# Moving 256 rows of the last weight onto other DMA engines in a single-core decode kernel

## The chip, the core and the metric

The kernel runs on one core of a Trainium2 chip. The core has five compute engines that the profile names: PE (TensorE, matrix multiplies; PEld is its weight load), DVE (VectorE), ACT (ScalarE), POOL (GpSimd) and SP (SyncE, here only used to issue DMAs). Sixteen DMA engines move data between HBM and the core's memory. A DMA load is issued by one compute engine's queue and is cut into packets, one per partition row here; the packets are spread over the DMA engines and each of these works its own share down.

The metric is the device time of one execution in microseconds (us). The median of three runs of the kernel before is 193.46 us (193.40 to 193.61).

## The reference

One token of eight sequences goes through an attention block with a cached window, and then through a small MLP block:

```python
x = A_x
h = x + _A_ref(_layernorm(x, axis=-1), A_k_cache, A_v_cache, A_wq, A_wo)
h2 = h + _B_ref(_layernorm(h, axis=-1), B_w1, B_w2, B_w3, B_w4)
```

`_A_ref` projects x (8 x 512) by wq (512 x 4096) to 32 heads, takes the last 2048 cached positions of K and V (8 sequences, 8 key heads, 128 wide, bf16), does a softmax attention and multiplies by wo (4096 x 512). `_B_ref` has a first part with w1 and w2 that shifts tokens; with one token the shifted terms are all zero, so what is left is

```python
h2 = _gelu(_layernorm(x1, axis=-1) @ w3) @ w4      # w3: 512 x 1792, w4: 1792 x 512
return x1 + h2
```

## The kernel before

Each compute engine has its own list of operations (class `Engine`, lines 39 to 70); `op` appends one with the semaphore values that it waits for. Order on an engine is the order of the Python calls; engines meet through semaphores alone. The helper `dma` (line 197) appends a load to an engine's list.

**Loads.** SP issues nearly everything, in one order: wq (4 MB), then 32 loads of 2 MB of K and V into a ring of 8 buffers, then wo in four loads of 1 MB (`sem_wo`), w3 in two of 896 KB, and w4 in four. A K or V load waits until the ring buffer that it overwrites was read (`taken`). w3 and w4 go into ring buffers as well (`w3_sb`, `w4_sb`, buffers W3S and W4S) and wait for `w_free`. Each load of 128 partitions puts eight packets on each of the sixteen DMA engines, and each engine works through SP's loads in order. w4 has 14 chunks of 128 rows, loaded as 8, 3, 2 and 1 chunks (`w4_chunks`, `w4_ends`, `sem_w4`). ACT issues one small load, x (line 215).

**Attention.** For each of 64 quarters PE transposes K (`pe_T`, L325), ACT and DVE copy the transposes out (L334, L336), PE forms the scores (`pe_QK`, L345). After eight quarters comes a softmax; POOL spreads the probabilities over four columns (L384), PE transposes them (L394), and multiplies by V (`pe_PV`, L445). The V product lags the scores by 20 quarters.

**Tail.** When the last V is used, PE reorders the result (L534), and `pe_wo` multiplies by wo in four steps, each of which waits for its load (L548). Between the steps `stream(n)` (L596) issues n multiplications whose result nobody reads. Then come sums over the features (L685 to L700), `pe_w3` in two halves (L710; second half waits for the second w3 load), a scaling on DVE (L738) and a gelu on ACT (L741), both in two parts of 8 and 6 chunks. `pe_w4` (L755) adds w4 chunk by chunk, as the four loads land, into an accumulator which `pe_fin` (L747) has opened. DVE and ACT copy out (L775, L776), and SP stores (L779).

**POOL's list.** It begins with memsets and an iota (L204 to L213), has the 30 spreads of L384, and ends with the memset `e_uz` of L684, which clears the buffer `uT` that pe_w3's operand is written into.

Of the kernel before, what the change touches and what calls it, by code (L numbers as in the profile page):

```python
# [11 lines left out]
B = 8  # L12
D = 512
# [9 lines left out]
FC = F // 128  # L23
KC = D // 128
EPS = 1e-5

NS = 8
NKT = 3
# [5 lines left out]
NWO = 4  # L34
# [33 lines left out]
def bass_sequential_preLN__sliding_block_cached__mixer_s_mlp__decode_kernel(  # L68
# [23 lines left out]
    with es:  # L92
        sb = lambda shape, dtype, name: es.enter_context(nc.sbuf_tensor(name, shape, dtype))
        ps_t = lambda shape, dtype, name: es.enter_context(nc.psum_tensor(name, shape, dtype))
        S = lambda name: es.enter_context(nc.semaphore(name))
# [4 lines left out]
        ident_b = sb([128, 128], dt.bfloat16, "ident_b")  # L100
# [7 lines left out]
        x_sb = sb([B, D], dt.bfloat16, "x_sb")  # L108
# [8 lines left out]
        QH, RW = H // 8, 8  # L117
# [4 lines left out]
        ring = sb([128, NS, NCQ * DH], dt.bfloat16, "ring")  # L122
        W3S, W4S = (2 * 2 * NB) % NS, (2 * 2 * NB + 1) % NS
        w3_sb = ring[:, W3S, 0:KC * F].rearrange("p (k f) -> p k f", k=KC)
        w4_sb = ring[:, W4S, 0:FC * D].rearrange("p (k n) -> p k n", k=FC)
        kT_sb = sb([128, NKT, 16 * 128], dt.bfloat16, "kT_sb")
# [3 lines left out]
        P4_sb = sb([128, 512, 4], dt.bfloat16, "P4_sb")  # L130
# [17 lines left out]
        half = sb([128, 2], dt.float32, "half")  # L148
# [19 lines left out]
        r2 = sb([128, B], dt.float32, "r2")  # L168
        xb = sb([128, NH], dt.float32, "xb")
        fin = sb([128, NH], dt.float32, "fin")  # L170
        uT = P4_sb[:, 0:64, :].rearrange("p (n w) k -> p n (w k)", n=KC)
        g_x = sb([128, FC * B], dt.float32, "g_x")
# [15 lines left out]
        oT_ps = sm[:, 480:512]  # L188

        sem_r = [S(f"sem_r{i}") for i in range(NS)]  # L190
        sem_wo = [S(f"sem_wo{i}") for i in range(NWO)]
        sem_x, sem_wq, sem_out = (S(n) for n in ("sem_x", "sem_wq", "sem_out"))
        sem_w3 = [S(f"sem_w3{i}") for i in range(2)]
        sem_w4 = [S(f"sem_w4{i}") for i in range(4)]
        PE, AC, DV, PO, SP = (Engine(S(n)) for n in ("s_pe", "s_act", "s_dve", "s_pool", "s_sp"))

        def dma(eng, dst, src, sem, *waits):
            def f(e):
                e.dma_start(dst, src).then_inc(sem, 16)  # L199
            eng.op(f, *waits, inc=False)  # L200


        X = (sem_x, 16)
        e_scr = PO.op(lambda e: e.memset(scratch[:], 1.0))  # L204
        PO.op(lambda e: e.memset(eps1[:], EPS))
        e_eps = PO.op(lambda e: e.memset(eps2[:], EPS * EPS))
        e_iota = PO.op(lambda e: e.iota(iota_f[:], [[1, 128]], base=0, channel_multiplier=-1,
# [4 lines left out]
        e_xz = PO.op(lambda e: e.memset(xlnT[:], 0.0))  # L212
        e_qz = PO.op(lambda e: e.memset(qwin[:], 0.0))  # L213
        e_warm = AC.op(lambda e: e.activation(scratch[:, 1:2], scratch[:, 0:1], ACT.Exp), e_scr)
        dma(AC, x_sb[:], A_x.rearrange("b s d -> (b s) d"), sem_x)

        e_idb = DV.op(lambda e: e.tensor_single_scalar(ident_b[:], iota_f[:], 0.0, ALU.is_equal), e_iota)
        e_idf = DV.op(lambda e: e.tensor_single_scalar(ident_f[:], iota_f[:], 0.0, ALU.is_equal))
# [324 lines left out]
        def pe_wo(n, *waits):  # L543
            def f(e):
                for q in range(n * (QH // NWO), (n + 1) * (QH // NWO)):
                    for r in range(RW):
                        for nb in range(KC):
                            ins = e.matmul(hT_ps[:, nb * NW:(nb + 1) * NW], wo_v[:, q, r, cols[nb]],  # L548
                                           oR_t[:, r * NW + q * B:(r + 1) * NW + q * B], start=(q == 0 and r == 0 and nb == 0),
                                           stop=(q == QH - 1 and r == RW - 1), skip_group_check=True)  # L550
                return ins
            e_wo.append(PE.op(f, (sem_wo[n], 16), e_exp[NB - 2], *waits))

        assert NG == 64 and LPV == 20
        at = {4 * (w + 1) + 2: w for w in range(SHARE)}
# [34 lines left out]
            if p >= 7 + LQK + 7 and (p - 7 - LQK - 7) % 8 == 0:  # L590
                softmax_5((p - 7 - LQK - 7) // 8)

        def stream(n):
            def f(e):
                for _ in range(n):
                    ins = e.matmul(O2_ps[:, :], ident_b[:, :], kT_sb[:, (NG - 1) % NKT, 0:512], start=True, stop=True)  # L596
                return ins
            if n:
                PE.op(f, e_acc[NV - 4])
# [37 lines left out]
        pick_rest(14, 1)  # L637
        finish(13)
        pick_rest(14, 2, 3)
        stream(4)  # L640
        pv(60)
        finish(14)
        pv(61, 62, 63)

        e_oR = reorder()
        stream(3)
        for n in range(NWO):
            pe_wo(n, e_oR, e_oz)
            stream((0, 4, 4, 1)[n])


        dma(SP, wq_v, A_wq.rearrange("(p k) n -> p k n", k=KC), sem_wq)
        for l in loads:
            what, b, j = l
            if what == "wo":
                n, qh = b, QH // NWO
                dma(SP, wo_v[:, n * qh:(n + 1) * qh].rearrange("p q r n -> p q (r n)"),
                    A_wo[n * qh * 128 * RW:(n + 1) * qh * 128 * RW, :].rearrange("(q p r) n -> p q (r n)", p=128, r=RW),
                    sem_wo[n], e_q)
                continue  # L660
            n = place[l]
            src = (A_k_cache if what == "k" else A_v_cache)[b, 4 * j:4 * (j + 1), W0:SK, :].rearrange(
                "h (p c) d -> p h (c d)", p=32)
            free = taken[quads[n - NS]] if n >= NS else None
            dma(SP, ring[:, n % NS, :], src, sem_r[n % NS], free)


        w_free = [taken[quads[n - NS]] for n in (len(quads), len(quads) + 1)]
        for a, sem in enumerate(sem_w3):
            dma(SP, w3_sb[:, 2 * a:2 * (a + 1), :].rearrange("p r f -> p (r f)"),  # L670
                B_w3[256 * a:256 * (a + 1), :].rearrange("(p r) f -> p (r f)", r=2), sem, w_free[0])

        FH = 8
        w4_chunks, w4_ends, f0 = [], [], 0
        for r, sem in zip((8, 3, 2, 1), sem_w4):
            lo = len(w4_chunks)
            w4_chunks += [slice(f0 + i, f0 + 128 * r, r) for i in range(r)]
            dma(SP, w4_sb[:, lo:lo + r, :].rearrange("p r n -> p (r n)"),
                B_w4[f0:f0 + 128 * r, :].rearrange("(p r) n -> p (r n)", r=r), sem, w_free[1] if lo == 0 else None)
            w4_ends.append(lo + r)  # L680
            f0 += 128 * r
        assert len(w4_chunks) == FC

        e_uz = PO.op(lambda e: e.memset(uT, 0.0), e_PT[LAST, 3])  # L684
        e_d = DV.op(lambda e: e.tensor_tensor(v3(hd[:, :]), hT, v3(xc[:, :]), ALU.add), e_wo[-1], e_xc[0])  # L685
        st1, st2 = sm[:, 0:NH], O_ps[:, 64:64 + NH]
        e_st1 = PE.op(lambda e: e.matmul(st1, ones_f[:, :], hd[:, :], start=True, stop=True), e_d)
# [12 lines left out]
        e_hc = DV.op(lambda e: e.scalar_tensor_tensor(v3(hc[:, :]), bc(msum), -1.0 / D, v3(hd[:, :]),  # L700
                                                      ALU.mult, ALU.add))

        y_ps, NY = [kbank[0], kbank[2]], (64, 32)

        def pe_w3(half, lo, hi, *waits):
            def f(e):
                for fc in range(lo, hi):
                    n, f = divmod(fc, FH)
                    for kc in (2 * half, 2 * half + 1):
                        ins = e.matmul(y_ps[n][:, f * NY[n]:(f + 1) * NY[n]], w3_sb[:, kc, w4_chunks[fc]],  # L710
                                       uT[:, kc, 0:NY[n]], start=(kc == 0 and f == 0), stop=(kc == KC - 1),
                                       skip_group_check=True)
                return ins
            return PE.op(f, *waits)
        pe_w3(0, 0, FC, e_u, (sem_w3[0], 16), e_scale[LAST, 1], e_acc[NV - 2])
        stream(1)
        e_y = [pe_w3(1, 0, FH, (sem_w3[1], 16)), pe_w3(1, FH, FC)]

        e = AC.op(lambda e: e.activation(s2[:, :], vsum[:, :], ACT.Sqrt, bias=eps2[:, :], scale=(1.0 + EPS) / D), e_vs)  # L719
        e1 = AC.op(lambda e: e.activation(s1[:, :], vsum[:, :], ACT.Sqrt, bias=eps1[:, :], scale=1.0 / D))  # L720
# [9 lines left out]
        def bcf(t, n):  # L730
            a = t[:, :]
            return bass.AP(tensor=a.tensor, offset=a.offset, ap=[a.ap[0], [0, n], [1, B]])

        e_gT = []
        for n in range(2):
            fn = (FH, FC - FH)[n]
            cs = slice(n * FH * B, (n * FH + fn) * B)
            e = DV.op(lambda e, n=n, cs=cs, fn=fn: e.tensor_tensor(v3(g_x[:, cs]),   # L738
                y_ps[n][:, 0:fn * NY[n]].rearrange("p (f w) -> p f w", w=NY[n])[:, :, 0:B], bcf(r2, fn),
                                                                   ALU.mult), e_y[n], e_r2)  # L740
            e_gT.append(AC.op(lambda e, cs=cs: e.activation(gT[:, cs], g_x[:, cs], ACT.Gelu_apprx_tanh), e))  # L741
        z_ps = S_ps[1]

        def rows(e, w, rhs, start=False, stop=False):
# [3 lines left out]
                               stop=stop, tile_position=(0, 64 * a), skip_group_check=True)  # L748
            return ins

        def pe_w4(lo, hi, *waits):
            def f(e):
                for fc in range(lo, hi):
                    for a in range(2):
                        ins = e.matmul(z_ps[64 * a:64 * a + B, 0:256], gT[:, fc * B:(fc + 1) * B],  # L755
                                       w4_sb[:, fc, 256 * a:256 * (a + 1)].rearrange("p (j r) -> p r j", r=2),
                                       start=False, stop=(fc == FC - 1), tile_position=(0, 64 * a), skip_group_check=True)
                return ins
            return PE.op(f, *waits)

# [4 lines left out]
            return ins  # L765

        PE.op(pe_fin, e_fin, e_exp[LAST], e_scale[LAST, 1])
        stream(2)
        for n, hi in enumerate(w4_ends):
            e_z = pe_w4(w4_ends[n - 1] if n else 0, hi, (sem_w4[n], 16), e_gT[0 if hi <= FH else 1])  # L770
        e_out = []
        for a in range(2):
            src = z_ps[64 * a:64 * a + B, 0:256].rearrange("p (r j) -> p r j", r=2)
# [3 lines left out]

        def store(e):
            e.dma_start(out.rearrange("b s d -> (b s) d"), out_sb[:, :]).then_inc(sem_out, 16)  # L779
            e.wait_ge(sem_out, 16)  # L780
        SP.op(store, *e_out, inc=False)

        for eng, e in ((nc.sync, SP), (nc.gpsimd, PO), (nc.scalar, AC), (nc.vector, DV), (nc.tensor, PE)):
# [29 lines left out]
```

## Time and profile before

| what | value |
|---|---|
| median of 3 runs | 193.46 us |
| the profiled execution's own time | 193.76 us |
| its span, first to last instruction | 192.3 us |
| clock granted to TensorE | 1.0 |
| HBM read | 79.18 MB, 412 GB/s over the span |
| PE busy | 159.8 us, 83% of the span |
| POOL busy | 35.8 us, 19% |

The span is shorter than the execution's time by 1.4 us, which lies outside of the first and last instruction. The views that are quoted below are: the page (its slices, its DMA queues, its chain), the chain of work that ended last in order of time, the timeline (start us, duration us, engine, line, operation, output from inputs, how many, and in brackets the idle time before with what ended it), and a table of stretches (busy us of each engine with the count of instructions, granted clock, share of the DMA engines that is busy, GB/s). Beside these views the trace holds a record of every DMA packet, with its start, duration, size and queue, but not the number of its DMA engine.

### The profile page before, as it was taken

How to read it: one execution, taken by the hardware profiler on the slowest of the kernel's cores; microseconds unless marked ns; L12 is line 12 of the kernel's file. 1: busy time of each engine (PE TensorE's matmuls, PEld its weight loads, DVE VectorE, ACT ScalarE, POOL GpSimd, SP SyncE). 2: the span in 40 equal slices, each digit the busy share in tenths (PEclk: the TensorE clock that was granted, in tenths of full speed). 3: DMA queues.
4: the chain of work that ended last, by engine and by line, in shares of the span. 5: the costliest groups of instructions: out<-in, count | busy, mean ns of one | idle time of the engine just before them, and what ended most of it. 6: DMA issues, size and time to landing. Idle time of an engine off the chain costs nothing.

```text
span 192.3 us, 4741 instructions
## 1 busy us (share of the span) xinstructions
PE 159.8 (83%) x2108; PEld 101.8 (53%) x2108; DVE 103.8 (54%) x256; ACT 84.4 (44%) x102; POOL 35.8 (19%) x44
## 2 busy tenths in 40 slices
PE   0028999789998989998999797979998998898795
PEld 0015767567665555655656464646565653366472
DVE  7702656367457654665475546554765456552050
ACT  5002776946744544454444532454445423530040
POOL 8000000350520080008000800052004402400000
PEclk9999999999999999999999999999999999999999
DMA  6999999999999999999999999999999999999992
GB/s 220 436 423 436 433 416 433 426 428 423 436 429 433 429 433 423 426 429 431 433 423 433 429 433 429 429 433 426 424 426 429 429 433 433 423 416 430 418 381 77
DMA packets 6244, 79.47 MB, mean 413 GB/s; under 512 B 705, under 2 KB 849, under 8 KB 1361
## 3 DMA queue, kind: packets, MB, share of 16 engines
q1 hardware_dynamic: 6208, 79.18, 97.0%
q8 instruction: 16, 0.26, 0.5%
q10 hardware_dynamic: 16, 0.01, 0.0%
q14 instruction: 4, 0.02, 0.0%
HBM read 79.18 MB, written 0.01 MB: 412 GB/s over the span
## 4 chain that ended last, share of the span: by engine, by line
DMA 78%; PE 16%; DVE 2%; SPq 2%; issue 1%; ACT 0%
DMA ring<-in_A_k_cache_dram 63%; DMA ring<-in_B_w_dram 16%; PE kT_ps L325 8%; PE O_ps L445 3%; PE S_ps L345 3%; SPq L199 2%; DVE kT_sb L336 1%; PE sm L394 1%; PE sm L496 1%; DVE pT_sb L407 1%; PE S_ps L755 0%; DVE mcol L356 0%; ACT P_sb L775 0%; PE sm L360 0%; PE sm L370 0%
## 5 line engine op out<-in xcount | busy, mean ns | idle before, releaser
L334 ACT ACTIVATE kT_sb<-kT_ps 128x1024 bf16<-128x1024 bf16 x64 | 65.2, 1023 | 65.4 <-PE kT_ps L325 65.4
L325 PE MATMUL kT_ps<-ident_p,ring 128*128 128x128 bf16 x1024 | 68.3, 220 | 9.0 <-DMA ring<-in_A_k_cache_dram 7.6
L336 DVE COPY kT_sb<-kT_ps 128x1024 bf16<-128x1024 bf16 x64 | 44.3, 692 | 48.9 <-PE kT_ps L325 48.9
L325 PEld LDWEIGHTS kT_ps<-ident_p,ring 128*128 128x128 bf16 x1024 | 57.7, 98 | 22.5 <-DMA ring<-in_A_k_cache_dram 10.5
L384 POOL TENSOR_TENSOR P_sb<-P_sb,mask_b 128x512 bf16<-128x512 bf16 x30 | 31.2, 1070 | 129.2 <-ACT P_sb L374 120.1
L445 PE MATMUL O_ps<-ring,pT_sb 128*64 128x512 bf16 x208 | 31.6, 390 | 0.0
L345 PE MATMUL S_ps<-kT_sb,qwin 128*32 128x512 bf16 x256 | 26.0, 390 | 0.0
L345 PEld LDWEIGHTS S_ps<-kT_sb,qwin 128*32 128x32 bf16 x256 | 6.8, 93 | 16.3 <-issue 14.4
L394 PE MATMUL sm<-ident_s,P_sb 128*128 128x128 bf16 x120 | 11.6, 219 | 2.0 <-DVE pT_sb L407 0.7
L407 DVE COPY pT_sb<-sm 128x512 bf16<-128x512 bf16 x28 | 11.6, 415 | 1.1 <-PE sm L394 1.1
L445 PEld LDWEIGHTS O_ps<-ring,pT_sb 128*64 128x64 bf16 x208 | 7.7, 108 | 6.1 <-issue 1.6
L394 PEld LDWEIGHTS sm<-ident_s,P_sb 128*128 128x128 bf16 x120 | 7.7, 97 | 4.5 <-issue 3.6
L480 DVE SCALAR_TENSOR_TENSOR acc<-O_ps,own_f,acc 128x128 f32<-128x128 f32 x24 | 8.4, 350 | 0.8
L268 PE MATMUL S_ps<-wbig,xlnT 128*32 128x512 bf16 x32 | 3.4, 596 | 5.3 <-DMA wbig<-in_A_wq_dram 5.3
L374 ACT ACTIVATE P_sb<-S_ps,negcol 128x512 bf16<-128x512 f32 x8 | 5.5, 687 | 3.0 <-DVE negcol L373 3.0
L254 PE MATMUL sm<-ident_b,xln_b 8*128 8x8 bf16 x4 | 0.3, 174 | 7.6 <-DVE xln_b L223 7.6
L496 PEld LDWEIGHTS sm<-sum_f,acc 128*128 128x128 f32 x20 | 3.0, 188 | 6.3 <-DVE pT_sb L407 3.3
L356 DVE TENSOR_REDUCE mcol<-S_ps 128x1 f32<-128x512 f32 x8 | 5.5, 689 | 1.5 <-PE S_ps L345 1.5
L480 DVE SCALAR_TENSOR_TENSOR iota_f<-O_ps,own_f,iota_f 128x128 f32<-128x128 f32 x15 | 5.2, 348 | 1.5 <-ACT iota_f L483 1.2
L596 PE MATMUL O_ps<-kT_sb,ident_b 128*128 128x512 bf16 x21 | 5.8, 379 | 0.0
L435 DVE TENSOR_TENSOR oT_all<-sm,rL 128x16 bf16<-128x16 f32 x15 | 3.4, 229 | 4.4 <-PE sm L496 4.3
L719 ACT ACTIVATE s<-vsum,eps 128x8 f32<-128x8 f32 x1 | 0.3, 301 | 11.8 <-DVE vsum L699 11.8
(123 smaller groups left out, 109.8 us busy)
## 6 DMA issues: line engine op xcount, KB each, us to landing
ring<-in_A_k_cache_dram SPq DMA_DIRECT2D x16, 2048.0 KB, 30.7
ring<-in_A_v_cache_dram SPq DMA_DIRECT2D x16, 2048.0 KB, 26.8
wbig<-in_A_wq_dram SPq DMA_DIRECT2D x1, 4096.0 KB, 12.3
wbig<-in_A_wo_dram SPq DMA_DIRECT2D x4, 1024.0 KB, 29.9
ring<-in_B_w_dram SPq DMA_DIRECT2D x2, 896.0 KB, 34.9
ring<-in_B_w_dram SPq DMA_DIRECT2D x1, 1024.0 KB, 32.1
ring<-in_B_w_dram SPq DMA_DIRECT2D x1, 384.0 KB, 30.3
ring<-in_B_w_dram SPq DMA_DIRECT2D x1, 256.0 KB, 30.5
```

The costliest lines, as they stand in the source:

```text
L325: ins = e.matmul(kT_ps[m % 3][:, c * 128:(c + 1) * 128], ring[:, s, n * DH:(n + 1) * DH], ident_p[:, :], is_transpose=True)
L334: e_lo[i] = AC.op(lambda e: e.activation(kT_sb[:, i % NKT, 0:1024], kT_ps[2 * i % 3][:, :], ACT.Copy), e_Tlo[i], e_QK.get(i - NKT))
L336: e_hi[i] = DV.op(lambda e: e.tensor_copy(kT_sb[:, i % NKT, 1024:2048], kT_ps[(2 * i + 1) % 3][:, :]), e_Thi[i], e_QK.get(i - NKT))
L345: ins = e.matmul(S_ps[b % 2][32 * h:32 * (h + 1), :], qwin[:, b, 4 * j + h, w0:w0 + 32], kT_sb[:, i % NKT, :].rearrange("p (c h k) -> p h ...
L356: e_max[b] = DV.op(lambda e: e.tensor_reduce(mcol[:, :], S_ps[b % 2][:, :], AX.X, ALU.max), e_QK[8 * b + 7], e_mT.get(b - 1))
L374: e_exp[b] = AC.op(lambda e: e.activation(P_sb[:, :], S_ps[j][:, :], ACT.Exp, bias=negcol[:, j:j + 1], scale=1.0, accum_out=lcol[:, j:j + 1]),
L384: e_sp[b, r] = eng.op(lambda e, r=r, pb=pb, mb=mb: e.tensor_tensor(P4_sb[:, 128 * r:128 * (r + 1), :], pb, mb, ALU.mult), e_exp[b], e_PT.g ...
L394: ins = e.matmul(buf[:, x * 128:(x + 1) * 128], P4_sb[:, 32 * c:32 * (c + 1), :].rearrange("p k h -> p (k h)"), ident_s[:, :], is_transpos ...
L407: e_pT[b, r] = DV.op(lambda e: e.tensor_copy(dst, pT_ps[:, :]), e_PT[b, r], free)
L445: ins = e.matmul(bank(w)[64 * t:64 * (t + 1), :], pT_sb[:, b % NB3, c, 64 * j:64 * (j + 1)], ring[:, s, :].rearrange("p (a c d) -> p c a d ...
L480: e_part[w] = eng.op(lambda e: e.scalar_tensor_tensor(dst, src, own, dst, ALU.mult, ALU.add), e_part[w], e_PV[4 * w + 3])
L596: ins = e.matmul(O2_ps[:, :], ident_b[:, :], kT_sb[:, (NG - 1) % NKT, 0:512], start=True, stop=True)
```

## The change

- **w4, first 128 rows.** Two loads issued by SP (`few(SP, ...)`), each of 64 rows to 8 partitions (8 rows of 1 KB, that is 8 KB, to a partition), with the source's outermost dimension 2, so that each runs on two DMA engines, numbers 0 and 1 by the change's words. They stand behind w3 and ahead of the rest of w4.
- **w4, next 128 rows.** One load issued by POOL (`few(PO, ...)`), 16 partitions of 8 KB, outermost dimension 4: four parts.
- **w4, the other 1536 rows** are loaded by SP as 5, 4, 2 and 1 chunks.
- The 256 rows lie in a ring buffer (`near_sb`) that POOL clears first (`e_nz`); all three loads wait for this memset. Their rows stand on other partitions than the gelu's output has them, so POOL builds selection matrices (`near`: a memset and three copies), `pe_near` (24 small multiplications) sorts the gelu's output, DVE copies it (`gn`), and 16 more multiplications use it with `near_sb`.
- pe_w3, the scaling and the gelu go in three parts (2, 5 and 7 chunks).
- x is loaded by POOL, as the second operation on its list.
- `stream` gets a width: 12, 12, 14, 16 and 4 multiplications of 128 columns stand where 4, 3, 4, 4 and 1 of 512 stood; 3 of 512 in place of 1 between the halves of w3; the 2 ahead of w4 are gone.
- Semaphores of early loads serve late ones again; there are 23 in place of 26.

```diff
-        sem_wo = [S(f"sem_wo{i}") for i in range(NWO)]
-        sem_x, sem_wq, sem_out = (S(n) for n in ("sem_x", "sem_wq", "sem_out"))
-        sem_w3 = [S(f"sem_w3{i}") for i in range(2)]
-        sem_w4 = [S(f"sem_w4{i}") for i in range(4)]
+        sem_x, sem_wq, sem_out, sem_wl, sem_w3l = (S(n) for n in ("sem_x", "sem_wq", "sem_out", "sem_wl", "sem_w3l"))
+        sem_w4l = [S(f"sem_w4{i}") for i in range(3)]
+        full = 16 * (4 * NB // NS)
+        NEAR = (4 * NB - 6) % NS
+        sem_wm = S("sem_wm")
+        w_wo = [(sem_wq, 32), (sem_out, 16), (sem_wl, 16), (sem_wm, 16)]
+        w_w3 = [(sem_r[W3S], full + 16), (sem_w3l, 16)]
+        sem_nw = S("sem_nw")
+        w_w4 = [(sem_r[W4S], full + 16)] + [(sem, 16) for sem in sem_w4l]
...
         e_scr = PO.op(lambda e: e.memset(scratch[:], 1.0))
+        dma(PO, x_sb[:], A_x.rearrange("b s d -> (b s) d"), sem_x)
...
-        dma(AC, x_sb[:], A_x.rearrange("b s d -> (b s) d"), sem_x)
...
-        stream(4)
+        stream(12, 128)
...
-        stream(3)
+        stream(12, 128)
         for n in range(NWO):
             pe_wo(n, e_oR, e_oz)
-            stream((0, 4, 4, 1)[n])
+            stream((0, 14, 16, 4)[n], 128)
...
+        NN, NT = 2, 3
+        side = ring[:, NEAR, :]
+        near_sb = side[:, 0:RW * D].rearrange("p (r n) -> p r n", r=RW)
+        near = side[:, RW * D:RW * (D + 32 * NT)].rearrange("p (r t n) -> p r t n", r=RW, t=NT)
+        e_nz = PO.op(lambda e: e.memset(near_sb, 0.0), taken["k", LAST, 1])
+        def few(eng, p, n, k, f, sem):
+            a = B_w4[f:f + n * RW, :]
+            dma(eng, near_sb[p:p + n].rearrange("p r n -> p (r n)"),
+                bass.AP(tensor=a.tensor, offset=a.offset, ap=[[RW * D, k], [k * RW * D, n // k], [1, RW * D]]), sem, e_nz)
+        few(PO, 64, 16, 4, 128, sem_nw)
+        e = PO.op(lambda e: e.memset(near, 0.0))
...
+        for t in range(2):
+            few(SP, 32 * t, 8, 2, 64 * t, sem_r[NEAR])
+        w4_chunks, w4_ends, f0 = [slice(128 * i, 128 * (i + 1)) for i in range(NN)], [], 128 * NN
+        for r, (sem, _) in zip((5, 4, 2, 1), w_w4):
...
-        e_uz = PO.op(lambda e: e.memset(uT, 0.0), e_PT[LAST, 3])
+        w3_parts = ((0, NN, 64), (NN, w4_ends[0], 64), (w4_ends[0], FC, 32))
+        e_uz = PO.op(lambda e: e.memset(P4_sb[:, 0:80, :], 0.0), e_PT[LAST, 3])
...
-        stream(1)
-        e_y = [pe_w3(1, 0, FH, (sem_w3[1], 16)), pe_w3(1, FH, FC)]
+        stream(3)
+        e_y = [pe_w3(1, n, w_w3[1]) for n in range(3)]
...
+        def pe_near(e):
+            for r in range(RW):
+                for t in range(NT):
+                    n = t // 2
+                    ins = e.matmul(gn_ps[32 * t:32 * (t + 1), r * B:(r + 1) * B], near[:, r, t, :], gT[:, n * B:(n + 1) * B],
+                                   start=True, stop=True, tile_position=(0, 32 * t), skip_group_check=True)
+            return ins
...
-        stream(2)
+        e = PE.op(pe_near, e_gT[0], e_near)
+        e_gn = DV.op(lambda e: e.tensor_copy(gn[0:32 * NT, :], gn_ps), e, e_uz)
         for n, hi in enumerate(w4_ends):
-            e_z = pe_w4(w4_ends[n - 1] if n else 0, hi, (sem_w4[n], 16), e_gT[0 if hi <= FH else 1])
+            e_z = pe_w4(gT, w4_sb, w4_ends[n - 1] if n else NN, hi, w_w4[n], e_gT[1 if n == 0 else 2])
+            if n == 0:
+                pe_w4(gn, near_sb, 0, RW, e_gn, (sem_r[NEAR], full + 32), (sem_nw, 16))
```

## The prediction

> **What bounds the kernel now.** The page first: its span, the slices of DMA, the queues, and the chain that ended last.
>
> ```profile
> span 192.3 us, 4741 instructions
> ...
> DMA  6999999999999999999999999999999999999992
> ...
> q1 hardware_dynamic: 6208, 79.18, 97.0%
> q8 instruction: 16, 0.26, 0.5%
> q10 hardware_dynamic: 16, 0.01, 0.0%
> q14 instruction: 4, 0.02, 0.0%
> ...
> DMA 78%; PE 16%; DVE 2%; SPq 2%; issue 1%; ACT 0%
> ```
>
> The DMA engines are full from the second slice to the last but one, and 78% of the chain is DMA. q1 is SP's loads, q10 is x, q8 and q14 fetch instructions. Next the end of the chain in order of time, then the timeline there.
>
> ```profile
> 159.31 30.47 DMA ring<-in_B_w_dram
> 189.78 0.04 issue
> 189.82 0.61 PE S_ps L755 x6
> 190.43 0.02 issue
> 190.45 0.45 ACT P_sb L775
> ```
>
> ```profile
> 185.57 1.45 PE L710 MATMUL kT_ps<-P_sb,ring 128*128 128x64 bf16 x28 [0.36 <-DMA ring<-in_B_w_dram]
> ...
> 187.99 0.77 PEld L755 LDWEIGHTS S_ps<-ring,gT 128*8 128x8 bf16 x16 [0.59 <-DMA ring<-in_B_w_dram]
> ...
> 189.20 0.21 PEld L755 LDWEIGHTS S_ps<-ring,gT 128*8 128x8 bf16 x6 [0.44 <-DMA ring<-in_B_w_dram]
> 189.82 0.09 PEld L755 LDWEIGHTS S_ps<-ring,gT 128*8 128x8 bf16 x4 [0.41 <-DMA ring<-in_B_w_dram]
> 190.13 0.09 PEld L755 LDWEIGHTS S_ps<-ring,gT 128*8 128x8 bf16 x2 [0.22 <-DMA ring<-in_B_w_dram]
> ```
>
> Each of w4's four loads is waited for; PE starts the last at 190.13. So the end is set by the DMA engine that delivers its share of w4 last. A table of stretches shows that not all are late:
>
> ```profile
> 186.00:186.50 0.50, 0.50 (x12) 0.50 (x11) 0.00 (x0) 0.00 (x0) 0.00 (x0) 1.00 1.02 404
> 186.50:187.00 0.50, 0.50 (x18) 0.47 (x18) 0.23 (x1) 0.00 (x0) 0.00 (x0) 1.00 0.60 242
> ...
> 187.50:188.00 0.50, 0.40 (x4) 0.01 (x4) 0.00 (x0) 0.05 (x1) 0.00 (x0) 1.00 0.52 197
> ...
> 188.50:189.00 0.50, 0.50 (x10) 0.21 (x6) 0.00 (x0) 0.00 (x0) 0.00 (x0) 1.00 0.49 182
> ```
>
> From 186.5 half of the engines (0.60, then 0.5) are idle. The packet records say which. On one engine a packet starts 3 or 4 ns before the last one ends, and 16 KB packets follow each other at 607 ns, so sixteen chains can be followed. Eight engines end at 186.36, 186.44, 186.47, 186.55, 186.62, 186.80, 187.12 and 188.02 us ("early"), eight at 189.27, 189.30, 189.32, 189.40, 189.40, 189.58, 189.60 and 189.70 ("late"). The late ones are exactly those that fetched two 16 KB blocks of q8 each, in rotation; one fetch holds its engine's own stream up by 1.41 us. PE's last start follows the last packet by 0.42 us (189.71 to 190.13).
>
> **The change part by part.**
>
> *Less w4 on every engine.* Packets follow at 305 ns (8 KB), 117 (3 KB), 80 (2 KB), 42 (1 KB); on the line between, 5 KB take 192 and 4 KB 155. Before, 8 x (305 + 117 + 80 + 42) = 4.35 us; after, 8 x (192 + 155 + 80 + 42) = 3.75 us. Each engine saves 0.61 us; the last late one would end at 189.70 - 0.61 = 189.09.
>
> *Two loads on engines 0 and 1.* Eight packets of 8 KB each: 8 x 305 ns plus two completions, 2.45 us. Are these two early? The records carry no engine number. But where two packets of different engines start in the same ns, an engine that carried a row of x is always listed ahead of one that did not, some twenty times; so the list seems to go by engine number there, with x on the lower eight. Among those, three early ones (186.36, 187.12, 188.02, in this order) are listed ahead of both late ones. The first two are then early: 186.36 to 187.12, less 0.61, plus 2.45, is 188.2 to 188.96, below 189.09. Cost nothing; late, they would end at 191.1 to 191.5.
>
> *SP's order.* Both loads and the rest of w4 behind them wait for POOL's memset. POOL's last spread ends at 163.78 + 1.48 = 165.26. The memset clears 4096 elements per partition; by the rows
>
> ```profile
> 1.59 3.29 POOL L213 MEMSET qwin<- 128x3840 bf16 x1
> ...
> 163.78 1.48 POOL L384 TENSOR_TENSOR P_sb<-P_sb,mask_b 128x512 bf16<-128x512 bf16 x1
> ...
> 167.43 0.31 POOL L684 MEMSET P_sb<- 128x256 bf16 x1 [2.17 <-PE kT_ps L394]
> ...
> 183.28 0.19 DVE L692 SCALAR_TENSOR_TENSOR P_sb<-msum,hd 128x32 bf16<-128x32 f32 x1
> ```
>
> it takes 3.5 us, to 168.8. Six issues of some 0.43 us follow (the w4 issues' shorter rows): 171.4. The first engine is through w3 at 181.97, so 10 us cover the wait.
>
> *POOL's list.* Behind the memset stand its load, a memset of 768 elements (0.66 us by the same rate), three copies (1.07 us at most each, by the spreads) and e_uz (0.4 us); even with 5 us for the load's issue, for which there is no row, it ends by 179, and its first reader is at 183.28.
>
> *POOL's load.* 4 x 8 KB on each of four engines, 32 KB. The trace has no load of POOL's, so I bound it. At SP's price it is 4 x 305 ns = 1.23 us per engine; as the packets of the fetch queues it would be dearer, since behind each 8 KB packet of q14 the engine's next packet took 240, 528 and 533 ns longer: 2.2 to 3.3 us. Nothing at the low end: if spread thinly over all sixteen engines it is 0.31 us each. I take 1.23: x's small packets on q10, the only data load of another queue here, left their neighbours' durations alone on most engines. What counts is where it falls. On an early engine (186.4 to 186.8) it ends at 187.0 to 187.4, unseen. On a late one 189.27 to 189.70 less 0.61 plus 1.23 is 189.9 to 190.32, later than now by up to 0.62 us. As it is issued near 169, it comes ahead of wo and w3 on its engines, so w3's second half could start about 1.0 us later (185.0 + 1.23 against 185.2); from there on the new order ends 0.5 to 0.6 later by itself, so the two hide each other.
>
> Four engines of sixteen, chosen without regard to the late eight, miss all of them once in 26 (70 of 1820), and as neighbours in the order above, with six of the eight without x late, in perhaps two of sixteen places. So I take the late engine.
>
> [...]
>
> *x by POOL.* x landed for DVE at 5.74, its product is ready at 9.93, and PE waits for wq until 13.18: 3.2 us of cover. POOL's iota and memsets move back by the issue; qwin's memset ends some 1 to 2 us after 4.88 and is needed at 18.1. Cost nothing; beyond the cover, PE starts later, but the ring has 8 buffers loaded ahead.
>
> *Streams.* 128 columns take 0.06 us a piece (16 transposes in 1.07), so 12 to 16 are shorter than the 1.02 us they replace, ahead of waits for wo (0.35 and 0.75 us). Three of 512 between w3's halves end at 185.5, just before the landing at 185.57.
>
> *Tail on PE.* w4 has 24 + 16 multiplications for 28, at 48 ns (16 in 0.77): +0.6 us, and pe_near 0.4 for the stream's 0.6; they fit between the landings. One more scaling and gelu (0.2 and 0.25) run beside w3's later chunks. If the landings came 0.61 earlier, PE would be at the last load by 189.55 against 189.51: just covered.
>
> *PE's fetches.* The tail gains about 160 PE instructions; 68 followed the sixteenth fetch, and fetches lie 260 records apart, so no seventeenth falls before the end. *Semaphores:* no row; at most they touch the 1.4 us outside the span. I take nothing.
>
> **Sum.** The last packet at 190.32 in place of 189.70: +0.62 on the profiled 193.76. That execution lies 0.30 above the median, so 193.46 + 0.62 = 194.1 us.
>
> **Rivals.**
> - *Early engines only (faster).* If all four of POOL's engines ended before 188.46 in the old run, their 0.62 more keeps them under 189.09; the end moves up by 0.58 (PE at 189.55): 192.9. The eight early engines speak for it, the count of places against. It decides at 188.46.
> - *Dear packets.* POOL's packets stall a late engine like a fetch, 1.0 to 2.1 us more: 195.1 to 196.2.
> - *Not four parts.* The load is spread over sixteen: -0.61 + 0.31 = -0.3, less any stall: 193.2 to 193.5.
> - *Engines 0 and 1 are late:* 191.1 to 191.5, 1.4 to 1.8 later: 194.9 to 195.3.
>
> **How the numbers follow.** Forecast 0.40, early only 0.28 (more than the places give, since nothing here shows how POOL's queue picks), dear 0.12, spread 0.15, 0 and 1 late 0.05. A measurement of this kernel can tell about 0.2%, 0.39 us. Faster: 0.28 and a little of the spread, 0.29. Slower: 0.36 of the forecast (its lower end, 0.2 us, is within 0.39), 0.12 and 0.05, 0.53. Same: 0.18. The range from 192.85 to 195.1 holds forecast, early and spread, 0.83; within the forecast alone it is 193.7 to 194.3.
>
> **What would show it.** Packet records of a new queue on four engines; those engines' ends against 189.09; the last L755 start near 190.75 with DMA as releaser; w3's second half near 186.5. It is wrong if the last L755 start is at 189.5 (early), if PE no longer waits for DMA there, or if q8's fetches take other engines.

## The result and the profile after

The changed kernel takes 195.23 us (median of 5 runs, 195.22 to 195.57), the kernel before 193.57 us beside it (193.40 to 193.62): a ratio of 1.0091, 95% interval 1.008 to 1.0102. The change costs 1.66 us. Slower was the likeliest sign in the prediction, but its time, 194.1 us, was 1.1 us short, and the measured time lies just above its range (192.85 to 195.1).

Of the 1.66 us, 1.4 lie within the span (193.7 us for 192.3) and some 0.2 outside of it. The page of the profile after, its span, the mean GB/s in forty slices, POOL's new queue (packets, MB, share) and the engines' shares of the chain:

```profile
span 193.7 us, 4909 instructions
...
GB/s 217 435 426 433 433 426 433 426 428 423 430 426 430 430 433 423 430 426 431 433 430 426 426 430 433 426 426 428 430 430 433 426 430 433 425 398 348 417 371 77
...
q0 software_dynamic: 112, 0.14, 0.2%
...
DMA 72%; PE 21%; DVE 4%; SPq 1%; issue 1%; ACT 1%
```

The DMA engines are as full as before, but in slices 36 and 37 (169 to 179 us) they move 398 and 348 GB/s where the neighbours have 417 to 433. Busy engines that move less: their packets have become longer. The timeline of the changed kernel shows what was issued then, and what came late (start, duration, engine, line, operation; idle time before in brackets):

```profile
165.37 3.54 POOL L679 MEMSET ring<- 128x4096 bf16 x1
...
168.94 4.30 SPq L204 DMA_DIRECT2D ring<-in_B_w_dram  x6
169.21 0.66 POOL L204 DMA_DIRECT2D ring<-in_B_w_dram  x1 [0.30 <-POOL ring L679]
...
186.84 0.17 PEld L739 LDWEIGHTS sm<-P_sb,ring 128*128 128x128 bf16 x4 [0.81 <-DMA ring<-in_B_w_dram]
...
189.28 0.43 PEld L794 LDWEIGHTS S_ps<-ring,gT 128*8 128x8 bf16 x10 [0.93 <-DMA ring<-in_B_w_dram]
...
191.47 0.09 PEld L794 LDWEIGHTS S_ps<-ring,gT 128*8 128x8 bf16 x2 [0.17 <-DMA ring<-in_B_w_dram]
```

POOL's load is issued at 169.2; w3's second half starts at 186.84 (185.57 before), w4's first product at 189.28 (187.99), its last at 191.47 (190.13). A table of stretches of the changed kernel (start:end, length, busy us and instructions of PE, its weight load, DVE, ACT and POOL, granted clock, busy share of the DMA engines, GB/s) narrows it down:

```profile
172.00:173.00 1.00, 0.80 (x26) 0.70 (x23) 0.51 (x2) 0.49 (x1) 0.00 (x0) 1.00 0.97 410
...
174.00:175.00 1.00, 0.68 (x38) 0.63 (x39) 0.41 (x2) 0.00 (x0) 0.00 (x0) 1.00 0.99 270
175.00:176.00 1.00, 0.54 (x12) 0.40 (x10) 0.79 (x2) 0.00 (x0) 0.00 (x0) 1.00 1.07 295
176.00:177.00 1.00, 0.92 (x32) 0.82 (x32) 0.00 (x0) 0.00 (x0) 0.00 (x0) 1.00 0.96 303
177.00:178.00 1.00, 0.27 (x10) 0.27 (x11) 0.00 (x0) 0.00 (x0) 0.00 (x0) 0.99 1.01 426
```

The kernel before, in the middle of that time:

```profile
174.00:175.00 1.00, 0.85 (x35) 0.51 (x35) 0.45 (x2) 0.00 (x0) 0.00 (x0) 1.00 0.97 410
175.00:176.00 1.00, 0.52 (x10) 0.23 (x9) 0.62 (x2) 0.00 (x0) 0.00 (x0) 1.00 1.09 459
```

The shares from 174 to 177 us are 0.96 to 1.07, about those of the kernel before, but the engines move 270 to 303 GB/s. The packet records agree. POOL's sixteen 8 KB packets run from 173.0 to 176.2 us; from about 173.4 to 176.9 us most 8 KB packets of wo, on **all sixteen** engines, take 430 to 600 ns in place of 309. Each engine loses about 1.07 us. (The granted clock falls to 0.5 from 178 to about 181.5 us in this execution. Another of the five held 1.0 on average and took 195.22 us, so the clock is not the loss.)

Followed back from the end, sixteen chains can be told apart again. The two that carry SP's small loads (called engines 0 and 1 as in the change; the records give no number) end at 190.81 and 191.14; the late ones end at 189.67 to 190.24, four early ones at 186.83 to 187.52. As far as packets can be followed through the slow stretch, POOL's 8 KB packets lie on engines 0 and 1 as well, four on the latter and at least two on the former, and four each on two other chains (ends 188.20 and 190.04). So engines 0 and 1 carry 96 KB ahead of their share of w4, and w4's first common load, 5 KB to a partition, is complete on them at 188.57 and 188.90, on all others by 188.00. The chain of work that ended last, in order of time, at its end:

```profile
170.47 18.77 DMA ring<-in_B_w_dram
189.28 2.49 PE S_ps L794 x40
191.79 0.45 ACT P_sb L817
```

From that landing on PE works its 40 products in 2.49 us, with one wait of 0.17 us.

Two things, then, that the prediction did not have: a slowing of all engines, and POOL's parts on engines that were already loaded.

### The profile page after: what moved, and what is told of

Same layout as the page of the kernel before. It is cut to its first block, busy times and chain, and to the rows that moved or that the text cites. A ratio compares the mean times of both kernels' runs of the same rounds, so it can differ in the third digit from the quotient of the medians.

```text
span 193.7 us, 4909 instructions
## 1 busy us (share of the span) xinstructions
PE 160.4 (83%) x2185; PEld 105.0 (54%) x2186; DVE 104.3 (54%) x258; ACT 84.7 (44%) x103; POOL 42.3 (22%) x51
## 4 chain that ended last, share of the span: by engine, by line
DMA 72%; PE 21%; DVE 4%; SPq 1%; issue 1%; ACT 1%
DMA ring<-in_A_k_cache_dram 62%; DMA ring<-in_B_w_dram 10%; PE kT_ps L330 8%; PE O_ps L450 4%; PE S_ps L350 3%; DVE kT_sb L341 1%; PE S_ps L794 1%; PE sm L501 1%; SPq L204 1%; PE kT_ps L450 1%; PE sm L399 1%; DVE P_sb L389 1%; DVE pT_sb L412 1%; ACT P_sb L379 0%; PE kT_ps L399 0%
## 5 line engine op out<-in xcount | busy, mean ns | idle before, releaser
L601 PE MATMUL O_ps<-kT_sb,ident_b 128*128 128x128 bf16 (+1 forms) x62 | 6.1, 255 | 0.1
```

What stands on the lines that cost most here:

```text
L601: ins = e.matmul(O2_ps[:, 0:w], ident_b[:, :], kT_sb[:, (NG - 1) % NKT, 0:w], start=True, stop=True)
```

## The experiments

**The same load by SP (e1), and no such load (e2).** Is it POOL's queue that slows the engines?

```diff
-        few(PO, 64, 16, 4, 128, sem_nw)
...
+        few(SP, 64, 16, 4, 128, sem_nw)
         for t in range(2):
             few(SP, 32 * t, 8, 2, 64 * t, sem_r[NEAR])
```

> The changed kernel with one edit: the load of the second 128 rows (16 partitions, 64 to 79, 8 KB each, source in four parts) is issued by SP, ahead of its other two small loads, in place of POOL. Same bytes, same destination, same place behind POOL's memset. In the changed kernel all sixteen DMA engines lost about 1.07 us between 173.4 and 176.9 us, while POOL's load was under way. Theory Q (POOL's queue is what slows them): the 8 KB packets of wo keep 309 ns beside this load, the late engines end near 188.7 to 189.1, and the end is set by engines 0 and 1, which still carry 96 KB more than before: 193.9 to 194.4 us. Theory P (the partitions 64 to 79 written from these four engines are what slows them): the same stretch of 430 to 600 ns packets appears, now behind w3, and the time stays at 195.0 to 195.4 us. If the slowdown is in both or in neither and engines 0 and 1 end early, my account of the end falls.

196.46 us (195.28 to 197.18), ratio 1.0145 (1.0097 to 1.0192). Stretches of that run, which lie behind w3 now:

```profile
181.00:182.00 1.00, 0.79 (x31) 0.77 (x31) 0.00 (x0) 0.00 (x0) 0.00 (x0) 1.00 1.05 442
...
183.00:184.00 1.00, 0.51 (x3) 0.06 (x3) 0.90 (x7) 0.03 (x1) 0.00 (x0) 1.00 0.99 199
184.00:185.00 1.00, 0.71 (x20) 0.74 (x21) 0.66 (x5) 0.98 (x3) 0.00 (x0) 1.00 0.96 244
```

The slowing has moved with the load: from 183 to 184.5 us 7 KB packets take mostly 540 to 586 ns for 272. It is not POOL's queue. The expectation by partitions had the stretch right and the time too low. The four executions lie apart, at 195.28, 195.79, 197.12 and 197.18 us. The profiled one is the longest; in it PE's last 40 products also took 3.96 us in place of 2.49, with the granted clock at 0.5 from 190 to 193 us. Why the clock fell there stays open, and so does whether the other long execution has the same cause.

```diff
-        NN, NT = 2, 3
+        NN, NT = 1, 2
-        few(PO, 64, 16, 4, 128, sem_nw)
-        for r, (sem, _) in zip((5, 4, 2, 1), w_w4):
+        for r, (sem, _) in zip((6, 4, 2, 1), w_w4):
```

> The changed kernel without the second 128 rows' load: SP's two small loads on engines 0 and 1 stay, the common loads of w4 hold 6, 4, 2 and 1 chunks, x stays with POOL. If POOL's load of w4 (its slowdown and its 32 KB on engines 0 to 3) is the whole loss, the late engines end at 189.70 - 0.30 = 189.4, engines 0 and 1 (186.4 to 187.1 before) at 188.5 to 189.3, and the time is 193.0 to 193.4 us, no slower than the kernel before. If the rest of the change costs as well (three parts of w3, sorting the gelu's output, streams, semaphores, x by POOL), it is 193.9 or more.

193.56 us (193.44 to 194.03), ratio 1.0004 (0.9995 to 1.0014). The span is 192.0, 0.2 to 0.3 under the one of before, as the bytes say; outside the span lie 1.48 us (median) where the kernel before has 1.33. So without that load the loss is gone, and a small gain within the span is eaten outside of it.

**Does x move POOL's parts? (e3)** In the changed kernel POOL loads x, eight rows, ahead of its load of w4. If its queue goes on from engine to engine, that moves the parts of w4; here x goes back to ACT.

```diff
-        dma(PO, x_sb[:], A_x.rearrange("b s d -> (b s) d"), sem_x)
...
+        dma(AC, x_sb[:], A_x.rearrange("b s d -> (b s) d"), sem_x)
```

> The changed kernel with one part undone: x is loaded by ACT again. Theory C (POOL's parts go to the engines that follow those of its last load, so that x moves them): without x they fall on other engines than with it, and the time changes by 0.3 us or more either way. Theory Z (they begin at the lowest engine whatever went before): the same four engines end last, and the time is that of the changed kernel, 195.1 to 195.3 us, less at most 0.2 us for what x by POOL does to the start.

195.37 us (195.04 to 195.53), ratio 1.0089 (1.0068 to 1.011), the time of the changed kernel; the slow stretch stands at the same place, and POOL's packets are again on the two chains that end last (190.77, 191.42). x by POOL did not move them.

**Which loads slow the engines? (e4, e5)** Probe loads in the middle of the kernel before, where only K and V stream:

```diff
+            a = B_w4[0:128, :]
+            four = [[RW * D, 4], [4 * RW * D, 4], [1, RW * D]]
+            at = {1: (PO, 64, 16, RW * D, four), 2: (PO, 0, 16, RW * D, four),
+                  3: (PO, 64, 16, RW * D, [[RW * D, 16], [1, RW * D]]), 4: (PO, 0, 128, D, [[D, 128], [1, D]]),
+                  5: (AC, 64, 16, RW * D, four)}.get(b)
```

> The kernel before, and in the free middle of its K and V stream five added loads of 128 KB that nobody reads, about 17 us apart: POOL in four parts to partitions 64 to 79; POOL in four parts to partitions 0 to 15; POOL in sixteen parts of one 8 KB row to partitions 64 to 79; POOL in 128 rows of 1 KB to 128 partitions; ACT in four parts to partitions 64 to 79. wo's loads wait for them. Bytes alone are 0.3 us more per load on the mean engine: 195.0 us if nothing else is lost. Theory Q (POOL's queue): the first four loads each show a stretch in which all engines' 8 KB and 16 KB packets take some 40% longer, the fifth does not. Theory P (partitions 64 to 79 from four engines): the first and the fifth show it, the second and fourth do not. Theory K (the small completion packets of POOL's loads, four on each engine): as Q, whatever the number of parts. If POOL's parts start where the last load's ended, the second load falls on other engines than the first.

200.16 us (one execution), span 198.8. Stretches in the second half of the first probe (61 to 63), in the second (78), the third (100 to 102), the fourth (120) and the fifth (136):

```profile
61.00:62.00 1.00, 1.00 (x20) 0.90 (x20) 0.56 (x1) 0.39 (x1) 0.00 (x0) 1.00 0.88 279
62.00:63.00 1.00, 1.00 (x12) 0.36 (x12) 0.73 (x2) 0.64 (x1) 0.00 (x0) 1.00 0.99 287
78.00:79.00 1.00, 0.90 (x10) 0.23 (x7) 1.00 (x3) 0.32 (x1) 0.00 (x0) 1.00 0.91 270
100.00:101.00 1.00, 0.90 (x11) 0.28 (x8) 0.96 (x4) 0.26 (x1) 0.00 (x0) 1.00 1.57 369
101.00:102.00 1.00, 0.24 (x4) 0.06 (x2) 0.93 (x3) 0.00 (x0) 0.00 (x0) 1.00 0.59 197
120.00:121.00 1.00, 0.90 (x12) 0.32 (x8) 0.96 (x4) 0.22 (x1) 0.00 (x0) 1.00 1.03 438
136.00:137.00 1.00, 1.00 (x20) 0.90 (x18) 0.23 (x1) 0.68 (x1) 0.00 (x0) 1.00 1.08 303
```

None of the three theories fits. Probes 1, 2, 3 and 5 slow the stream (16 KB packets mostly at 700 to 1400 ns for 611), POOL's and ACT's, on partitions 64 to 79 and on 0 to 15, in four parts and in sixteen; only the fourth, to all 128 partitions, does not. (The third is short; its two stretches move 283 GB/s on average.) That left two readings: too few partitions (theory F of what follows), or the wrong engines for them (theory D: the same partitions can be written without loss from some engines and not from others). In the next run all five loads go in four parts to 16 partitions, and only their destinations and issuers vary:

```diff
-            at = {1: (PO, 64, 16, RW * D, four), 2: (PO, 0, 16, RW * D, four),
-                  3: (PO, 64, 16, RW * D, [[RW * D, 16], [1, RW * D]]), 4: (PO, 0, 128, D, [[D, 128], [1, D]]),
-                  5: (AC, 64, 16, RW * D, four)}.get(b)
+            at = {1: (PO, 0, 16, RW * D, four), 2: (PO, 16, 16, RW * D, four), 3: (PO, 64, 16, RW * D, four),
+                  4: (PO, 64, 16, RW * D, four), 5: (AC, 0, 16, RW * D, four)}.get(b)
```

> The kernel before with five added loads of 128 KB that nobody reads, all in four parts of 4 partitions x 8 KB, at the places of the first probe run; only the destinations differ: POOL to partitions 0-15, POOL to 16-31, POOL to 64-79, POOL to 64-79 again, ACT to 0-15. In the first probe run all four loads of 8 KB rows to 16 partitions slowed every engine (16 KB packets at 800 to 1300 ns for 611), whichever queue issued them, and the one to all 128 partitions did not. Theory F (any load that puts many rows on few partitions slows all): all five slow the stream again, 199.5 to 200.5 us. [...] If POOL's four parts also move on by four engines with each load (0-3, 4-7, 8-11, 12-15), the first three are harmless and the fourth is slow: about 0.3 us a load for bytes and 1 us for the slow one, 195.5 to 196.5 us. [...]

196.26 us (one execution), span 194.9. Stretches of the first probe (61 to 63), the second (78), the third (97), the fourth (119) and the fifth (137):

```profile
61.00:62.00 1.00, 1.00 (x18) 0.95 (x17) 0.61 (x2) 0.28 (x1) 0.00 (x0) 1.00 1.01 426
62.00:63.00 1.00, 1.00 (x12) 0.30 (x10) 0.69 (x1) 0.74 (x1) 0.00 (x0) 1.00 1.07 451
78.00:79.00 1.00, 0.81 (x15) 0.82 (x16) 0.93 (x4) 0.15 (x1) 0.00 (x0) 1.00 0.96 410
97.00:98.00 1.00, 0.90 (x10) 0.34 (x8) 0.96 (x4) 0.05 (x1) 0.00 (x0) 1.00 1.04 442
...
119.00:120.00 1.00, 0.00 (x0) 0.00 (x0) 0.00 (x0) 0.00 (x0) 0.00 (x0) 1.00 1.07 311
137.00:138.00 1.00, 0.66 (x8) 0.40 (x6) 0.51 (x3) 0.00 (x0) 0.00 (x0) 1.00 1.02 434
```

In probes 1, 2, 3 and 5 both the probe's 8 KB packets (309 ns) and the stream's (median 611) are undisturbed; in the fourth the stream's median, from 116 to 122 us, is 807. Probes 3 and 4 are the same load, issued twice: the same rows of w4, the same partitions 64 to 79, at another place within the partitions' rows. What can differ besides is the engines, and the packet records show that they do: followed as chains, the parts of the first three probes lie on three sets of four engines that have none in common, and the fourth's begin on the remaining four, as far as two pairs of chains that run in step can be told apart. So POOL's parts move on by four engines at each load, and as far as these runs show it is the engines that decide. The two runs agree on this: POOL's four-part load to 64 to 79 slowed the stream as the first (e4) and as the fourth (e5), but not as the third; to 0 to 15 it did as the second (e4), but not as the first. ACT's slowed it on 64 to 79 (e4), but not on 0 to 15 (e5). That is theory D, and the time, 196.26 us, lies in the range of 195.5 to 196.5. That range took for granted which engines go with which partitions; what the runs show are these loads, slow and not slow, and no run shows why. Below, the engines of POOL's first load are counted as 0 to 3, those of its third as 8 to 11. The cost: five probes of 0.31 us of bytes (128 KB at 425 KB/us) and one slow one make 194.9 - 192.2 = 2.7, so 1.2 us for the slow one; in e4, with four slow ones, 198.8 - 192.2 - 1.5 = 5.1, 1.3 each.

**The changed kernel with POOL's parts eight engines on (e8).** Two small loads of POOL's ahead of it, four parts each, move its parts on to engines 8 to 11, from which e5 wrote the partitions 64 to 79 without loss:

```diff
         e_qz = PO.op(lambda e: e.memset(qwin[:], 0.0))
+        for t in range(2):
+            dma(PO, P4_sb[16 * t:16 * (t + 1), 0:128, :].rearrange("p k h -> p (k h)"),
+                bass.AP(tensor=B_w4[:, :].tensor, offset=B_w4[:, :].offset, ap=[[D, 4], [4 * D, 4], [1, D]]), sem_dm)
```

> The changed kernel with one addition: at the start, behind its memsets, POOL issues two loads of 16 KB in four parts (16 partitions x 1 KB, to partitions 0-15 and 16-31 of a buffer that is still unused; nobody reads them). [...] Theory D: no engine is slowed from 173 to 177 us (8 KB packets stay at 309 ns), engines 0 and 1 lose their third 32 KB and end below 189.2, and of engines 8 to 11 the late ones end at 189.09 to 190.3. That is the likeliest case of my prediction, with some 0.2 us more outside the span for x by POOL: 193.9 to 194.5 us, 0.8 to 1.3 under the changed kernel. If the order of parts has nothing to do with it, the time stays at 195.1 to 195.4.

194.04 us (193.81 to 194.23), ratio 1.0027 (1.0015 to 1.0039): 1.2 us come back. The stretches of this run, as above of the changed kernel:

```profile
174.00:175.00 1.00, 0.85 (x41) 0.80 (x42) 0.45 (x2) 0.00 (x0) 0.00 (x0) 1.00 1.05 442
175.00:176.00 1.00, 0.54 (x16) 0.40 (x12) 0.61 (x2) 0.00 (x0) 0.00 (x0) 1.00 0.97 410
176.00:177.00 1.00, 0.75 (x30) 0.65 (x26) 0.00 (x0) 0.00 (x0) 0.00 (x0) 1.00 1.00 418
```

Every packet of POOL's took 309 ns, and so did wo's, but for one behind a code fetch. Engines 0 and 1 end at 188.63 and 189.03; five of the late ones at 188.81 to 188.91, and three at 189.98, 190.01 and 190.14, 1.24 us (four packets of 309 ns) above 188.9 at most. The chain's end:

```profile
170.30 18.04 DMA ring<-in_B_w_dram
188.38 2.46 PE S_ps L798 x40
190.87 0.45 ACT P_sb L821
```

This is the case that the prediction took for the likeliest, at about its time: 0.53 us above the kernel before, for a forecast of 0.62. The last packet, at 190.14, is where the sum has it (189.9 to 190.32). But PE does not wait for it. PE starts at 188.38, when the first common load is complete on the last of POOL's four engines (187.90; by 186.79 on the others), and its 40 products then last until 190.84. That the two ways come out alike is luck. What remains, 0.5 us, is POOL's 32 KB on engines that are late, by way of that first landing.

**What can be had (e7, e9 to e12), and the time outside the span (e6).** First the two loads with x back on ACT, and x alone moved in the kernel before:

```diff
-        dma(AC, x_sb[:], A_x.rearrange("b s d -> (b s) d"), sem_x)
...
         e_scr = PO.op(lambda e: e.memset(scratch[:], 1.0))
+        dma(PO, x_sb[:], A_x.rearrange("b s d -> (b s) d"), sem_x)
```

> The kernel before with one part of the change: x is loaded by POOL, as the second operation on its list. x lands some 2.5 us later, covered by wq. The span stays at 192.0 to 192.4 us. The run with only the two loads of SP had a span 0.3 us under the one of before and the same time, so some 0.15 to 0.2 us more lay outside the span. Theory X (that is POOL's load of x): the time outside the span is 1.45 us or more here and the median 193.65 to 193.8. Theory Y (something else of the change): 1.3 us outside, 193.45 to 193.6.

> The changed kernel without POOL's load of the second 128 rows (common loads of 6, 4, 2 and 1 chunks), and with x loaded by ACT again: of the change SP's two loads on engines 0 and 1, the three parts of the MLP's first product, the sorting of the gelu's output, the streams and the semaphores are left. The span is that of the run with x by POOL, 191.9 to 192.1. Theory X: 1.3 us outside, 193.2 to 193.35 us, faster than before by 0.1 to 0.2%. Theory Y: 1.47 outside, 193.45 to 193.6 us.

e6 (the diff above, on the kernel before): 193.74 us (193.62 to 193.85), ratio 1.0009 (0.9999 to 1.0018), span 192.2, 1.54 us outside (median). e7 (e2 with that edit undone): 193.31 us (193.15 to 193.55), ratio 0.9989 (0.9979 to 0.9998), span 192.0, 1.33 outside. Both agreed with theory X; later runs did not (below).

Then the same 256 rows by SP in two loads of four parts, to partitions 0 to 15 (which e5 wrote without loss from POOL's first four engines) and 32 to 47, and the first 128 alone, to 0 to 15; all on engines 0 to 3, with no load of POOL's:

```diff
-        few(PO, 64, 16, 4, 128, sem_nw)
...
-        for t in range(2):
-            few(SP, 32 * t, 8, 2, 64 * t, sem_r[NEAR])
+        for t in range(NT):
+            few(SP, 32 * t, 16, 4, 128 * t, sem_r[NEAR])
```

with NN, NT = 2, 2 (e9), and with 1, 1 and common loads of 5, 4, 3 and 1 chunks (e10); x by ACT in both.

> [...] The common loads keep 5, 4, 2 and 1 chunks. Theory D: nothing is slowed; the engines that fetch code end at 189.1, engines 0 and 1 at 188.2 to 188.9, engines 2 and 3 (with the q14 fetches, 187.1 and 188.0 before) at 189.0 to 189.9; 192.8 to 193.6 us. If moving 256 rows costs time by itself (the MLP's three parts, the sorting, PE's longer tail), it is over 193.8.

> Half of that: only the first 128 rows, by SP in four parts to partitions 0-15 (engines 0 to 3, 32 KB each), x by ACT, common loads of 5, 4, 3 and 1 chunks. The late engines end at 189.70 - 0.31 - 0.08 = 189.3 (a row of 6 KB goes as 4 + 2, so 5, 4, 3, 1 costs less than 6, 4, 2, 1), engines 0 to 3 below 189.0; PE's last product no longer waits for DMA. 193.1 to 193.4 us, as the run with two loads and x by ACT, 193.31.

e9: 193.96 us (193.74 to 195.59), ratio 1.0031 (1.0012 to 1.0051). The engines did what was expected: nothing is slowed, the four end at 188.35, 188.36, 188.96 and 189.85, the others by 189.10. The time did not, because of PE:

```profile
187.99 0.73 PE L790 MATMUL S_ps<-ring,gT 128*8 128x256 bf16 x10 [0.61 <-DMA ring<-in_B_w_dram]
188.56 1.07 PE L790 MATMUL S_ps<-ring,P_sb 128*8 128x256 bf16 x16
189.47 1.01 PE L790 MATMUL S_ps<-ring,gT 128*8 128x256 bf16 x14
190.20 0.09 PEld L790 LDWEIGHTS S_ps<-ring,gT 128*8 128x8 bf16 x2 [0.19 <-DMA ring<-in_B_w_dram]
```

The slowest of the four delivers w4's first common load at 187.61; PE starts at 187.99 and needs 2.5 us for 40 products, to 190.48, later than the 190.43 of before. One weight load waits 0.19 us for the last common load, which adds 0.04 us at most: e8's 40 products take 2.46 us with no such wait. (The profiled execution is the fastest of e9's ten, 193.74 us; what the others add has no trace.) The small loads lie ahead of that landing on their engines, and the landing starts PE's last chain.

e10: 193.60 us (193.38 to 193.80), ratio 1.0003 (0.9994 to 1.0013); the span is 191.9, the time outside 1.61, which undoes it. Against the expectation PE's last products still wait for DMA, for 0.35 us ahead of 189.25 and 0.15 ahead of 189.61.

Last, e7 with 5, 4, 3 and 1 chunks, and e10 with x by POOL:

```diff
-        for r, (sem, _) in zip((6, 4, 2, 1), w_w4):
+        for r, (sem, _) in zip((5, 4, 3, 1), w_w4):
```

> The fastest so far (SP's two loads of 64 rows on engines 0 and 1, x by ACT, 193.31 us) with common loads of 5, 4, 3 and 1 chunks in place of 6, 4, 2 and 1. A row of 6 KB goes as 4 + 2 KB, 159 + 84 ns for 196, so each engine saves 8 x (159 + 84 + 84 - 196 - 121) = 0.08 us. Span 191.8 to 191.9 (192.0 before the edit). If the time outside the span stays at 1.33, 193.1 to 193.25 us; if it is a property of each program that these edits do not explain, up to 193.5.

> The run with 128 rows in four parts of SP's and a span of 191.8 to 192.2 us had 1.62 us outside the span, with x by ACT. Here only x is moved to POOL. Theory X (x by POOL adds 0.2 us outside the span): 1.8 us outside, 193.75 to 193.9. Theory Y (it is something else of each program, such as where its code lies): anything from 1.3 to 1.6, 193.2 to 193.7.

e11: 193.21 us (193.13 to 194.19), ratio 0.9987 (0.9978 to 0.9997), span 191.9: the fastest here, by 0.13%, which is less than the 0.2% that the prediction put down as the limit of a measurement, though the interval excludes 1. The reason that e10 and e11 were given, a row of 6 KB that goes as 4 KB and 2 KB, is a misreading: in e2 and e7 these rows went as packets of 6 KB in 234 ns, and the 4 KB and 2 KB packets are those of the next two loads. By the durations 6, 4, 2 and 1 KB take 523 ns and 5, 4, 3 and 1 KB take 522, so nothing is saved there. What differs in e11 is that the first common load is smaller, and PE starts on w4 at 187.18 us for 187.48 in e7. Its chain's end:

```profile
171.12 18.17 DMA ring<-in_B_w_dram
189.34 0.64 PE S_ps L791 x8
190.00 0.45 ACT P_sb L814
```

PE waits for DMA until 189.34 and then has eight products left: with fewer bytes to wait for, its 42 products are next, so there is little left in this direction.

e12: 193.31 us (193.21 to 194.60), ratio 0.9997 (0.9984 to 1.0009), span 191.9, 1.36 outside. Moving x to POOL *lowered* the time outside the span here, by 0.25, and raised it by 0.21 in e6. Theory X falls. The medians by run: 1.53 in the changed kernel, 1.55 (e1), 1.48 (e2), 1.57 (e3), 1.54 (e6), 1.61 (e10), and 1.31 to 1.36 in the kernel before and in e4, e5, e7, e8, e9, e11 and e12, with x by POOL and by ACT in both groups. What makes it stays open; it is 0.2 of the 1.66 us.

## Why the prediction was wrong, and where it was right

*The bound.* Right that the last delivery of w4 sets the end, and that some engines are late. Incomplete in one term: it took PE's 40 products at 48 ns each, 1.9 us, "just covered". They take 2.46 to 2.50 us, 62 ns each, so it is not the last landing but the first common one, plus 2.5 us, that ends e8, e9 and the changed kernel; the waits of 0.17 and 0.19 us for the last load in the latter two add 0.04 at most. It also makes the faster rival too good: e7, with no load of POOL's at all, starts PE on w4 at 187.48 and ends only 0.4 us before the old end.

*Less w4 on every engine, two loads on engines 0 and 1.* Right, though the saving that it puts at 0.61 us is 0.60 by its own terms. In e8 the five late engines without POOL's packets end at 188.81 to 188.91 (forecast: 189.09 for the last), engines 0 and 1 at 188.63 and 189.03 (188.2 to 188.96).

*SP's order, POOL's list, x, streams.* Right that they are covered. The memset took 3.54 us (3.5); SP's six issues 4.30 us, not 2.6, to 173.24, still 9.8 us before the first engine is through w3 (183.04); x landed for DVE at 8.42 and PE still waited for wq, with its first product at 13.38 for 13.21. e7 holds the tail's edits, with a smaller sorting, and has a shorter span than before.

*PE's fetches.* Wrong, a seventeenth q8 block came at 189.91. e7 and e11 have one as well (189.1) and end earlier than before.

*POOL's load.* This is the step that failed, in both its parts. **Where it falls:** the prediction took a late engine at four packets, by the count of the late ones. The load began on engine 0: two parts on engines that already carried 64 KB. In e5 POOL's queue goes four engines on at each four-part load, and e8 agrees; x, with its eight rows, did not move it (e3, e8). **What it costs:** 1.23 us on its own engines was right (1.24 in e8), but only from engines 8 to 11. From those it ran on in the changed kernel it slowed all sixteen, by about 1.07 us each. The row the price was taken from, x's packets on q10, left its neighbours alone, but those were 1 KB each, not 128 KB to 16 partitions. The two parts are one mistake here: on engines 8 to 11 neither would have come.

On engines 0 and 1 both add up: 1.07 us of slowing and 1.24 of packets, 188.90 for the first common landing against 187.90 at most in e8; from there PE gives 0.9 us at the end, and 0.2 lie outside the span. Taken one at a time, the first landing would be the other engines' 188.00 with the slowing alone, and 188.90 - 1.07 = 187.83 with the packets alone, so either would cost about as much as e8's parts; that is worked out, not run.

*The rivals.* "Dear packets" holds the measured time, 195.23 within 195.1 to 196.2, at a chance of 0.12, but for another reason: it had one late engine stalled, and here all sixteen were slowed and the end was set by engines that had been early. "Engines 0 and 1 are late" holds it as well (194.9 to 195.3, a chance of 0.05) and named the right engines, again with the wrong cause: they were early, and POOL's parts and the slowing made them late. The rest were not what happened.

## What to carry to other kernels

Beside a stream that keeps all engines busy, 128 KB to the same 16 partitions cost 0.31 us of bytes from some DMA engines and 1.1 to 1.3 us more on every engine from others, whoever issued it. No view before the change told which, so probe engine and partitions together before pricing such a load. A load that is to run on early engines still lies ahead of what comes behind it there: price it at the first wait that starts the last chain, not at the last packet. And a price taken from a neighbouring row is worth only as much as that row shares the property in question; here the size was looked at and the destination was not.

## What the runs showed of the hardware that was not expected

- Loads to sixteen partitions slowed all sixteen DMA engines, not only those that carried them, in the changed kernel, e1, e3, e4 (all four) and e5 (one of five): 7 KB packets at 540 to 586 ns for 272, 8 KB at 430 to 600 for 309, 16 KB mostly at 700 to 1400 for 611, for about as long as the load runs (3.5 to 5 us in four parts, about 2 in sixteen). From other engines a load to the same partitions slowed none (16 KB at 611 ns in e5, 8 KB at 309 in e8). What makes the difference no run shows.
- Behind the strong slowing e3 shows a weaker one: 8 KB packets at about 342 ns for 309, from 177 to 179 us. The changed kernel does not have it, and no run explains it.
- POOL's four-part loads moved on by four engines each in e5 and e8; x, eight rows, left the parts of w4 where they were without it.
- Rows of 5, 6 and 7 KB each went as one packet, in 196, 234 and 272 ns.
- The time outside the span is about 1.33 us in some programs and 1.48 to 1.61 us in others, and x's queue does not decide which.
